# The last step of an inverse transform: one float32 product, or three float32r products of split operands

## The chip, the cores and the metric

The kernel runs on one core of one Trainium2 chip. The core has a matrix engine (TensorE, in the profile PE, with its weight loads shown apart as PEld), a vector engine (DVE), a scalar engine (ACT), GpSimd (POOL) and a sync engine (SP) that here only issues transfers. They run beside each other and wait for each other by semaphores; each works through its own queue in order. The metric is the device time of one execution in microseconds. Before the change it is 2467.11 us, the median of three runs (2465.29 to 2468.96).

## The reference

```python
X = np.fft.rfft(x, axis=1)                 # x: 8 batches x 3008 x 256
Y = X * (filt_r + 1j * filt_i)[None]
y = np.fft.irfft(Y, n=3008, axis=1).astype(np.float32)
t = y.reshape(8 * 3008, 256)
h = t @ w_in                               # 256 x 2048
g = h * (1.0 / (1.0 + np.exp(-1.702 * h)))
out = g @ w_out                            # 2048 x 256
```

A long convolution along the sequence, by a Fourier transform, is followed by a feed-forward block over all 24064 rows.

## The kernel before

The transform of length 3008 = 64 x 47 is done by small matrix products: a step over 64 points, a step over 47 points, the product with the filter, and the two steps back. The 47-point steps read and write the 64-point ones through DRAM, since the data are turned between them. The feed-forward block works on tiles of 512 rows (384 in some tiles that end a batch), six tiles a batch.

The first batch is transformed alone, in float32 (`first_fft`). From then on two things run at once. `mlp(b, t, y, nb)` does the feed-forward block of a tile in 16 steps, one for each 128 of the 2048 hidden channels: six products into a PSUM tile `h` (`first`, line 537), two activations on ACT (`g` and `gh`, lines 541 and 542), a difference on DVE (`gl`, line 543) and six products into two PSUM tiles `o` (`second`, line 551). All of these are float32r products of operands split into a high and a low part, so that each product of two float32 matrices is three float32r products: high by high, low by high, high by low. Beside it a generator `fft(b + 1)` does the transform of the next batch up to the last inverse step, in small pieces handed out between the steps of `mlp`; it is split into high and low parts in the same way, with `mm3` for the three products, and with its steps over 47 points at lines 442 to 445.

The last inverse step, over 64 points, is `signal(b, t, y)`. It makes one tile `y`, already split into high and low, for `mlp`. From the second batch on it loads `br` (128 partitions x 4 x 256) from DRAM (`b_d`, two transfers, one for each half of the partitions). For each half `m` of the 256 columns of `br` it then does four products into one PSUM tile `i1`, one for each of the four pieces of 128 columns, with the table `t2_sb` of 128 x 128 as the moving operand and the piece of `br` as the weights, in float32. In a batch's last tile the fourth product has only 64 rows and 64 columns (line 510). ACT then copies `i1` to the high part of `y` and DVE subtracts to get the low part. In the first batch `br` comes from an on-chip tile `b_t` by four transposes instead of a load.

`signal` yields after each half. The main loop, at the end of the file, advances it after the steps 3 and 9 of the tile before (11 and 13 where that tile ends a batch), and the load goes out with the first half. That order is what the program is written in; a scheduler then orders each engine's queue from it, other than the parts pinned with `keep_in_program_order`, and often moves a half of `signal` as much as two tiles ahead of its use. Tiles in SBUF come from rotating pools: `raw` (six buffers) holds `br` as well as the inputs and intermediate results of `fft`.

Of the kernel before, what the change touches and what calls it, by code (L numbers as in the profile page):

```python
# [9 lines left out]
F32 = mybir.dt.float32  # L10
F32R = mybir.dt.float32r
# [3 lines left out]
ALU = mybir.AluOpType  # L15

B, S, D, DFF = 8, 3008, 256, 2048
N1, N2 = 64, 47
NS = 32
NH = 24  # L20
P = 128
# [129 lines left out]
def tile_kernel(  # L151
# [9 lines left out]
    nc = tc.nc  # L161
    const = ctx.enter_context(tc.tile_pool(name="const", bufs=1))
# [7 lines left out]
    def raw(name):  # L170
        return sb.tile([P, 4, D], F32, tag="raw", name=name, bufs=6)
# [6 lines left out]
    def load_in(dst, src):  # L178

        ins = nc.sync.dma_start(dst, src)  # L180
        if in_order[0]:
            tc.keep_in_program_order(ins)


    tab = const.tile([P, sum(WIDTHS.values())], F32, name="tab")
    t1_sb = const.tile([P, 2, P], F32R, name="t1_sb")
    de_sb = const.tile([Q, 2, 4, Q], F32R, name="de_sb")
    HALF = NFC // 2
    table, at = {}, 0
# [3 lines left out]
    t2_sb, sign = table["t2"], table["sign"]  # L193
# [70 lines left out]
                todo[i - 4].send(to)  # L264
            yield

    b_of, stores, done_w = {}, [], [0]

    zy = []

    def mm3(ps, wh, wl, mh, ml):
        nc.tensor.matmul(ps, wh, mh, start=True, stop=False)  # L272
        nc.tensor.matmul(ps, wh, ml, start=False, stop=False)  # L273
        nc.tensor.matmul(ps, wl, mh, start=False, stop=True)  # L274
# [10 lines left out]
    def split_de():  # L285

        pin = tc.keep_in_program_order
        de_f = table["de"].rearrange("p (m c) -> p m c", m=4)  # L290
        pin(nc.scalar.copy(t1_sb[:, 0], table["t1"]))
        pin(nc.vector.tensor_tensor(t1_sb[:, 1], table["t1"], t1_sb[:, 0].bitcast(F32), ALU.subtract))
        pin(nc.gpsimd.memset(de_sb.bitcast(F32), 0.0))
        for k in range(2):
            h, o = slice(64 * k, 64 * k + 48), slice(64 - 64 * k, 112 - 64 * k)
            pin(nc.scalar.copy(de_sb[h, k, :, h], de_f[h, :, h]))
            pin(nc.vector.tensor_tensor(de_sb[h, k, :, o], de_f[h, :, h], de_sb[h, k, :, h].bitcast(F32), ALU.subtract))
            pin(nc.gpsimd.tensor_copy(de_sb[o, k], de_sb[h, k].bitcast(F32)))
# [190 lines left out]
    def signal(b, t, y):  # L489

        if b:
            br = raw(f"br_{b}_{t}")
            for j in range(2):
                n = NH * j + 4 * t
                load_in(br[64 * j : 64 * j + 64], b_of[b][n : n + 4].rearrange("n k d -> k n d"))
            br = [br[:, :, P * m : P * m + P] for m in range(2)]
        full = 4 if t < 5 else 3
        for m in range(2):
            if b == 0:
                ps = ps_f.tile([P, 4, P], F32, tag="f", name=f"bt_{t}_{m}")  # L500
                for i in range(4):
                    q = 4 * (4 * t + i)
                    nc.tensor.transpose(ps[:, i], b_t[:, m, q : q + 4].rearrange("p c s -> p (c s)"), table["eye"])
                br = {m: sb.tile([P, 4, P], F32, tag="half", name=f"br_{b}_{t}_{m}", bufs=4)}
                (nc.vector.tensor_copy if m else nc.scalar.copy)(br[m], ps)
            ps = ps_f.tile([P, 512], F32, tag="f", name=f"i1_{b}_{t}_{m}")
            for i in range(full):
                nc.tensor.matmul(ps[:, P * i : P * i + P], br[m][:, i], t2_sb, start=True, stop=True)  # L508
            if full == 3:
                nc.tensor.matmul(ps[:, 384:448], br[m][0:64, 3], t2_sb[0:64, 0:64], start=True, stop=True)  # L510
            w = P * full
            to = [(y, 0, w, 0)]
            if full == 3:
                to.append((carry, 0, 64, 384) if b % 2 == 0 else (y, 448, 64, 384))
            for dst, o, w, q in to:
                nc.scalar.copy(dst[:, 0, m, o : o + w], ps[:, q : q + w])
                nc.vector.tensor_tensor(dst[:, 1, m, o : o + w], ps[:, q : q + w], dst[:, 0, m, o : o + w].bitcast(F32), ALU.subtract)
            if full == 3 and b % 2:
                nc.gpsimd.tensor_copy(y[:, :, m, 384:448], carry[:, :, m, :].bitcast(F32))  # L519
            yield  # L520
# [47 lines left out]
    def store():  # L568

        if stores:  # L570
            nc.sync.dma_start(*stores.pop(0))

    def run(gen, n=None):
        while n is None or n > 0:
            if next(gen, run) is run:
                return False
            n = None if n is None else n - 1
        return True


    carry = const.tile([P, 2, 2, 64], F32R, name="carry")
    b_t = const.tile([P, 2, 96, NS], F32, name="b_t")
    ys = {}

    def start(b, t):
        ys[b, t] = sb.tile([P, 2, 2, 512], F32R, tag="y", name=f"y_{b}_{t}")
        return signal(b, t, ys[b, t])
# [7 lines left out]
    for i, (b, t) in enumerate(tiles):  # L595
        if t == 0:

            done, chunk, chunks = 0, 0, 6 * NFC - (18 if b == 0 else 8)
            nxt = fft(b + 1) if b + 1 < B else iter(())
        nb = 4 if t < 5 or b % 2 else 3  # L600
        sig = start(*tiles[i + 1]) if i + 1 < len(tiles) else iter(())
        for fc, _ in enumerate(mlp(b, t, ys.pop((b, t)), nb)):
            if fc == 0:
                store()
            if i == 0:
                run(w_parts, 1)
                if fc == 9:
                    split_de()
                    in_order[0] = False
            if i or fc >= 10:  # L610
                chunk += 1
                while chunk <= chunks and done < STEPS * chunk // chunks:
                    run(nxt, 1)
                    done += 1
            if fc in ((11, 13) if t == 5 else (3, 9)):
                run(sig, 1)
        run(sig)
        if i == 0:
            zy.append(const.tile([P, 4, 2, 2, D], F32R, tag="zy", name="zy"))
            nc.gpsimd.memset(zy[0][32:64].bitcast(F32), 0.0)  # L620
# [29 lines left out]
```

## Time and profile before

| | |
|---|---|
| median of three runs | 2467.11 us |
| profiled execution | 2467.57 us, of which the span from the first to the last instruction is 2465.7 |
| granted clock of TensorE, mean | 0.992 |
| transfers | 246.60 MB, 100 GB/s on average |
| matmuls and weight loads | 11082 each |
| transfers that load `br` | 84, median 4.6 us from issue to landing |

The page gives busy time of each engine, then the chain of work that ended last, then groups of equal instructions. In a row of a group stand the line, the engine, the operation, what it writes and reads, its shape and count; behind the first bar its busy time and the mean length of one; behind the second the idle time of its engine just ahead of it, and who ended most of that idle time. In a row of the timeline stand start and length in microseconds, the engine, the line, the operation and the number of instructions merged into the row. Rows of waits read: who waited for whom, total, times, longest. Rows of windows give a stretch, its length, the busy time of each engine (PE, PEld, DVE, ACT, POOL, with counts), the granted clock, and share and rate of transfers.

### The profile page before, as it was taken

To read this page: it belongs to the slowest core of one execution; us is meant where nothing else is said; L and a number is where in the kernel's file an instruction comes from. 1 tells how busy PE (TensorE), PEld (TensorE's weight loads), DVE (VectorE), ACT (ScalarE), POOL (GpSimd) and SP (SyncE) were. 2 spreads that over 40 slices of the span, in tenths; PEclk is the share of its full clock that TensorE was granted. 3 is DMA by queue.
4 is the path that set the end of the run, shared out by engine and by line. 5 is a ranking of instruction groups with operands and counts; after the bars stand their busy time and mean duration, and the time that the engine had idled before them with its cause. 6 is when DMAs were issued, how large, how long until landed. Compare 5 with 4: busy or idle time off the path is not lost.

```text
span 2465.7 us, 31786 instructions
## 1 busy us (share of the span) xinstructions
PE 2398.9 (97%) x11082; PEld 1986.8 (81%) x11082; DVE 1538.4 (62%) x2167; ACT 1313.0 (53%) x2441; POOL 824.3 (33%) x714
## 2 busy tenths in 40 slices
PE   7789999999999999999999999999999999999999
PEld 6568778877888888988887887988888888898887
DVE  6856884488638883578735786368753788422222
ACT  5555565555555555555554555556555555444443
POOL 4743552355214432344323443234422354000000
PEclk9799999999999999999999999999999999999999
DMA  9335334544345434534344343444335443300000
GB/s 281 95 97 129 92 96 132 132 115 115 91 150 110 100 88 115 142 93 103 96 136 106 93 100 92 137 103 116 88 94 141 100 98 85 70 16 9 18 9 18
DMA packets 140927, 246.60 MB, mean 100 GB/s; under 512 B 15584, under 2 KB 81248, under 8 KB 140768
## 3 DMA queue, kind: packets, MB, share of 16 engines
q1 hardware_dynamic: 62528, 133.72, 19.6%
q10 hardware_dynamic: 53152, 66.80, 10.3%
q0 software_dynamic: 25088, 44.05, 9.2%
q8 instruction: 88, 1.44, 0.2%
q14 instruction: 71, 0.58, 0.1%
HBM read 150.67 MB, written 93.85 MB: 99 GB/s over the span
## 4 chain that ended last, share of the span: by engine, by line
PE 78%; DVE 7%; DMA 5%; issue 2%; ACT 2%; POOL 1%; SPq 1%; ACTq 1%; POOLq 0%; DVEq 0%
PE o L551 35%; PE h L537 35%; PE i L508 3%; DVE gl L543 2%; DMA br<-b_d 2%; PE s L445 2%; PE i L445 2%; DMA x<-in_x_dram 1%; DVE c_buf L396 1%; DMA zy<-a_d 1%; DMA b_d<-b 1%; POOL c_buf L389 1%; PE s L272 1%; PE s L274 1%; PE s L273 1%
## 5 line engine op out<-in xcount | busy, mean ns | idle before, releaser
L537 PE MATMUL h<-y,wi 128*128 128x512 f32 (+1 forms) x4608 | 1172.9, 387 | 2.8 <-ACT gh L542 1.6
L543 DVE TENSOR_TENSOR gl<-g,gh 128x512 fp32r<-128x512 f32 (+1 forms) x768 | 657.2, 858 | 737.7 <-ACT gh L542 653.3
L537 PEld LDWEIGHTS h<-y,wi 128*128 128x128 f32 x4608 | 862.8, 188 | 173.3 <-ACT gh L542 2.5
L541 ACT ACTIVATE g<-h 128x512 f32<-128x512 f32 (+1 forms) x768 | 452.5, 589 | 909.7 <-PE h L537 795.6
L551 PE MATMUL o<-gh,wo 128*128 128x512 f32 (+1 forms) x3072 | 832.5, 390 | 10.9 <-ACT gh L542 9.1
L551 PEld LDWEIGHTS o<-gh,wo 128*128 128x128 f32 x3072 | 571.0, 189 | 130.5 <-ACT gh L542 15.1
L551 PE MATMUL o<-gl,wo 128*128 128x512 f32 (+1 forms) x1536 | 479.9, 388 | 8.9 <-DVE gl L543 8.8
L542 ACT ACTIVATE gh<-h 128x512 fp32r<-128x512 f32 (+1 forms) x768 | 448.5, 585 | 51.4 <-PE o L551 46.5
L460 POOL TENSOR_TENSOR zy<-c_buf,zy 48x512 fp32r<-48x512 f32 x224 | 334.4, 1493 | 96.7 <-DVE zy L459 87.2
L551 PEld LDWEIGHTS o<-gl,wo 128*128 128x128 f32 x1536 | 285.4, 188 | 68.7 <-DVE gl L543 14.6
L389 POOL TENSOR_TENSOR c_buf<-c_buf,u_buf 112x512 f32<-112x512 f32 x128 | 185.2, 1447 | 457.9 <-DVE c_buf L388 456.8
L409 POOL TENSOR_TENSOR xl<-x,xh 128x512 fp32r<-128x512 f32 x84 | 112.3, 1349 | 424.9 <-ACT xh L408 392.9
L428 POOL DMA_DIRECT2D zy<-a_d x224 | 128.3, 575 | 279.6 <-PE s L445 74.9
L396 DVE TENSOR_TENSOR c_buf<-s,c_buf 48x512 f32<-48x512 f32 x224 | 154.1, 688 | 29.4 <-ACT c_buf L395 23.4
L396 DVE TENSOR_TENSOR b<-i,b 48x512 f32<-48x512 f32 x224 | 154.0, 687 | 7.8 <-ACT b L395 1.4
L395 ACT COPY c_buf<-s 48x512 f32<-48x512 f32 x224 | 130.2, 581 | 24.7 <-PE s L445 13.4
L395 ACT COPY b<-i 48x512 f32<-48x512 f32 x224 | 130.1, 581 | 20.8 <-DVE b L396 6.3
L459 DVE CAST zy<-c_buf 48x512 fp32r<-48x512 f32 x224 | 94.2, 421 | 51.9 <-POOL c_buf L389 47.9
L508 PEld LDWEIGHTS i<-tab,br 128*128 128x128 f32 x736 | 101.1, 194 | 26.0 <-issue 8.8
L508 PE MATMUL i<-tab,br 128*128 128x128 f32 x736 | 105.7, 280 | 11.3 <-DMA br<-b_d 7.8
L519 POOL CAST y<-carry 128x128 fp32r<-128x128 f32 x8 | 2.8, 378 | 263.8 <-PE h L537 263.6
L387 DVE TENSOR_TENSOR u_buf<-c_buf,f_buf 48x512 f32<-48x512 f32 x112 | 87.6, 782 | 3.6
(88 smaller groups left out, 1263.4 us busy)
## 6 DMA issues: line engine op xcount, KB each, us to landing
f_buf<-fs SPq DMA_DIRECT2D x224, 192.0 KB, 3.4
zy<-a_d POOLq DMA_DIRECT2D x224, 192.0 KB, 3.6
x<-in_x_dram SPq DMA_DIRECT2D x48, 512.0 KB, 4.8
out_dram<-out SPq DMA_DIRECT2D x44, 512.0 KB, 3.6
a_d<-ah ACTq DMA_DIRECT2D x84, 256.0 KB, 3.5
a_d<-al ACTq DMA_DIRECT2D x84, 256.0 KB, 3.9
b_d<-b ACTq DMA_DIRECT2D x112, 192.0 KB, 2.5
br<-b_d SPq DMA_DIRECT2D x84, 256.0 KB, 4.6
```

The costliest lines, as they stand in the source:

```text
L389: nc.gpsimd.tensor_tensor(u1, u1, u2, ALU.add)
L395: nc.scalar.copy(dst[h], ps[k][o])
L396: nc.vector.tensor_tensor(dst[h], ps[k][h], dst[h], ALU.add)
L409: nc.gpsimd.tensor_tensor(xl, src, xh.bitcast(F32), ALU.subtract)
L428: nc.gpsimd.dma_start(zy[0][64 * k : 64 * k + 48, i % 2].rearrange("p k s d -> p k (s d)"), src.rearrange("n k s d -> n k (s d)"),)
L460: nc.gpsimd.tensor_tensor(y[o, k], u1[h], y[h, k].bitcast(F32), ALU.subtract)
L508: nc.tensor.matmul(ps[:, P * i : P * i + P], br[m][:, i], t2_sb, start=True, stop=True)
L537: nc.tensor.matmul(ps[:, :w], wi_sb[half][:, wk, kc, c], y[:, yk, kc, :w], start=n == 0, stop=n == 5)
L541: nc.scalar.activation(g[:, :w], ps[:, :w], AF.Gelu_apprx_sigmoid)
L542: nc.scalar.activation(gh[:, :w], ps[:, :w], AF.Gelu_apprx_sigmoid)
L543: nc.vector.tensor_tensor(gl[:, :w], g[:, :w], gh[:, :w].bitcast(F32), ALU.subtract)
L551: nc.tensor.matmul(pos[m][:, :w], wo[:, wk, P * m : P * m + P], gp[gk][:, :w], start=fc == 0 and n == 0, stop=fc == NFC - 1 and n == 2,)
```

## The change

From the second batch on, `signal` splits `br` into a high part (a copy to float32r on ACT) and a low part (a subtraction on POOL), for each half of the columns, into `b_hl`, a tile with two places that alternate from tile to tile and that takes the memory of `b_t` once the first batch is done. The table `t2` is split once in the same way (`t2_hl`, in `split_de`). Each of the four products is then `mm3`, three float32r products with 128 columns of the moving operand. In the last tile of a batch the fourth product now uses all 128 rows, and 64 columns, in every batch; in the first batch the products stay float32. `signal` yields once more, behind the load and the split, and the main loop advances it after steps 1, 5 and 9 (9, 12 and 14 where the tile ends a batch).

```diff
+    t2_hl = const.tile([P, 2, P], F32R, name="t2_hl")
...
-        pin(nc.scalar.copy(t1_sb[:, 0], table["t1"]))
-        pin(nc.vector.tensor_tensor(t1_sb[:, 1], table["t1"], t1_sb[:, 0].bitcast(F32), ALU.subtract))
+        for t, name in ((t1_sb, "t1"), (t2_hl, "t2")):
+            pin(nc.scalar.copy(t[:, 0], table[name]))
+            pin(nc.vector.tensor_tensor(t[:, 1], table[name], t[:, 0].bitcast(F32), ALU.subtract))
...
-            br = [br[:, :, P * m : P * m + P] for m in range(2)]
+            if not b_hl:
+                b_hl.append(const.tile([P, 2, 2, 4, D], F32R, tag="b_t", name="b_hl"))
+            hl = b_hl[0][:, t % 2]
+            for m in range(2):
+                ms = slice(P * m, P * m + P)
+                nc.scalar.copy(hl[:, 0, :, ms], br[:, :, ms])
+                nc.gpsimd.tensor_tensor(hl[:, 1, :, ms], br[:, :, ms], hl[:, 0, :, ms].bitcast(F32), ALU.subtract)
+        yield
...
-            for i in range(full):
-                nc.tensor.matmul(ps[:, P * i : P * i + P], br[m][:, i], t2_sb, start=True, stop=True)
-            if full == 3:
-                nc.tensor.matmul(ps[:, 384:448], br[m][0:64, 3], t2_sb[0:64, 0:64], start=True, stop=True)
+            for i in range(4):
+                w = P if i < full else 64
+                if b:
+                    ms = slice(P * m, P * m + P)
+                    mm3(ps[:, P * i : P * i + w], hl[:, 0, i, ms], hl[:, 1, i, ms], t2_hl[:, 0, :w], t2_hl[:, 1, :w])
+                else:
+                    nc.tensor.matmul(ps[:, P * i : P * i + w], br[m][:, i], t2_sb[:, :w], start=True, stop=True)
...
-    b_t = const.tile([P, 2, 96, NS], F32, name="b_t")
+    b_t = const.tile([P, 2, 96, NS], F32, tag="b_t", name="b_t")
...
-            if fc in ((11, 13) if t == 5 else (3, 9)):
+            if fc in ((9, 12, 14) if t == 5 else (1, 5, 9)):
```

Two places show how the instructions stand. The first is PE's queue where the first half of tile (5, 3), that is `i1_5_3_0`, is made, during the feed-forward block of tile (5, 0). Before, with `h` and `o` the two parts of that block and `gh`, `gl` the operands of the second part (batch, tile and step are the first three numbers of a name):

```order
L537 MATMUL h_5_0_15_14357<-y_5_0_13595,wi_1_840 128x512 x6
L551 MATMUL o_5_0_0_13959<-gl_5_0_13_14310,wo_1_841 128x512
L551 MATMUL o_5_0_1_13960<-gl_5_0_13_14310,wo_1_841 128x512
L508 MATMUL i1_5_3_0_14991<-tab_74,br_5_3_14988 128x128 x4
L445 MATMUL i2_6_2_0_15018<-zy_1189,de_sb_76 112x512
```

Now, during the second step of tile (5, 1):

```order
L274 MATMUL i1_5_3_0_15586<-t2_hl_76,b_hl_3367 128x128
L275 MATMUL i1_5_3_0_15586<-t2_hl_76,b_hl_3367 128x128
L273 MATMUL i1_5_3_0_15586<-t2_hl_76,b_hl_3367 128x128
L549 MATMUL h_5_1_2_14955<-y_5_1_14462,wi_0_499 128x512 x6
L274 MATMUL i1_5_3_0_15586<-t2_hl_76,b_hl_3367 128x128
L275 MATMUL i1_5_3_0_15586<-t2_hl_76,b_hl_3367 128x128
L447 MATMUL s2_6_4_0_15620<-zy_1192,de_sb_77 112x512
```

Four float32 products have become twelve float32r products, mostly in one row and here with the six products of a step of `mlp` ahead of the last two; they stand four steps of `mlp` later than before, still well ahead of tile (5, 3).

The second place is where the split of the same `br` stands, in the queues of ACT and POOL. On ACT, where before step 9's activations of tile (5, 0) followed step 8's:

```order
L541 ACTIVATE g_5_0_8_14168<-h_5_0_8_14161 128x512
L542 ACTIVATE gh_5_0_8_14169<-h_5_0_8_14161 128x512
L541 ACTIVATE g_5_0_9_14197<-h_5_0_9_14190 128x512
L542 ACTIVATE gh_5_0_9_14198<-h_5_0_9_14190 128x512
L395 COPY c_buf2_81<-s2_6_2_0_14836 48x512
```

two copies now stand between them:

```order
L554 ACTIVATE gh_5_0_8_14685<-h_5_0_8_14677 128x512
L503 CAST b_hl_3367<-br_5_3_15474 128x4x128 x2
L553 ACTIVATE g_5_0_9_14713<-h_5_0_9_14706 128x512
L554 ACTIVATE gh_5_0_9_14714<-h_5_0_9_14706 128x512
L397 COPY c_buf2_82<-s2_6_2_0_15380 48x512
```

On POOL, two subtractions now stand between the differences of the transform's filter step (`c_buf`, `zy`) and its loads from DRAM:

```order
L391 TENSOR_TENSOR c_buf1_81<-c_buf1_81,u_buf1_84 112x512
L462 TENSOR_TENSOR zy_1192<-c_buf1_81,zy_1192 48x512 x2
L504 TENSOR_TENSOR b_hl_3367<-br_5_3_15474,b_hl_3367 128x4x128 x2
L430 DMA zy_1192<-a_d6_14517 48x2x512 x2
L391 TENSOR_TENSOR c_buf2_82<-c_buf2_82,u_buf0_83 112x512
```

What ACT and POOL do behind these rows now waits for the load of `br`, which before only PE waited for.

More of the change, by code (lines that the diff above doesn't have):

```diff
@@ L265, in weights @@
             yield
-    b_of, stores, done_w = {}, [], [0]
+    b_of, b_hl, stores, done_w = {}, [], [], [0]
     zy = []
```

## The prediction

> **What bounds the kernel now.** I read the page first, from the top: busy time by engine, the chain, the groups.
>
> ```profile
> span 2465.7 us, 31786 instructions
> PE 2398.9 (97%) x11082; PEld 1986.8 (81%) x11082; DVE 1538.4 (62%) x2167; ACT 1313.0 (53%) x2441; POOL 824.3 (33%) x714
> PE 78%; DVE 7%; DMA 5%; issue 2%; ACT 2%; POOL 1%; SPq 1%; ACTq 1%; POOLq 0%; DVEq 0%
> L508 PEld LDWEIGHTS i<-tab,br 128*128 128x128 f32 x736 | 101.1, 194 | 26.0 <-issue 8.8
> L508 PE MATMUL i<-tab,br 128*128 128x128 f32 x736 | 105.7, 280 | 11.3 <-DMA br<-b_d 7.8
> ```
>
> PE is busy 97% of the span and holds 78% of the chain; every other engine has a third of its time or more free. So the question is how many nanoseconds of PE's queue a product takes, and only then who makes PE wait. The waits of PE and of ACT, and the three stages (first transform, body, last batch without transform work), come next.
>
> ```profile
> 0.00:75.00 75.00, 55.78 (x333) 44.27 (x334) 52.04 (x78) 39.69 (x83) 37.81 (x31) 0.91 0.79 239
> 75.00:2115.00 2040.00, 1998.75 (x9146) 1651.05 (x9145) 1388.76 (x1942) 1129.00 (x2086) 785.97 (x682) 0.99 0.43 108
> 2115.00:2465.00 350.00, 344.35 (x1607) 291.44 (x1605) 97.60 (x148) 144.34 (x273) 0.53 (x2) 1.00 0.08 23
> PE o L551 <- ACT gh L542: 9.1, 8, 2.8
> PE i L508 <- DMA br<-b_d: 7.8, 11, 1.5
> ACT g L541 <- PE h L537: 795.6, 595, 5.4
> PE i L445 <- POOL zy L460: 0.8, 1, 0.8
> ```
>
> From 75 us on PE idles 41 us in 2040 and 6 in 350. What is added to PE's queue there is added to the time, nearly one for one. The changed step itself waits for its own load 11 times, 7.8 us in all. ACT, in turn, waits for PE 795.6 us.
>
> **What a product costs on PE.** Mean durations are no use here: records of 280 ns overlap, since eight of them begin within 0.89 us. What counts is the step from one start to the next, read in the timeline (start, length, engine, line, count).
>
> ```profile
> 1119.48 0.97 PEld L508 LDWEIGHTS i<-tab,br 128*128 128x128 f32 x8 [0.72 <-DVE gl L543]
> 1120.37 0.18 PEld L445 LDWEIGHTS s<-zy,de_sb 112*112 112x112 f32 x1
> 1126.93 0.63 PE L445 MATMUL s<-zy,de_sb 112*112 112x512 f32 x2
> 1127.39 1.07 PE L551 MATMUL o<-gh,wo 128*128 128x512 f32 x4
> 1128.31 2.88 PE L537 MATMUL h<-y,wi 128*128 128x512 f32 x12
> 1131.03 0.62 PE L551 MATMUL o<-gl,wo 128*128 128x512 f32 x2
> 1040.20 0.28 PE L442 MATMUL i<-zy,de_sb 112*112 112x256 f32 x1
> 1040.32 0.28 PE L443 MATMUL i<-zy,de_sb 112*112 112x256 f32 x1
> 1040.43 0.28 PE L442 MATMUL i<-zy,de_sb 112*112 112x256 f32 x1
> 1040.55 0.28 PE L443 MATMUL i<-zy,de_sb 112*112 112x256 f32 x1
> 1040.67 1.09 PE L551 MATMUL o<-gh,wo 128*128 128x512 f32 x4
> ```
>
> The four float32 products of one call (four rows of columns) stand in the trace as eight pairs of weight load and matmul: a float32 product is two pairs. Eight loads take 1120.37 - 1119.48 = 0.89 us, 0.111 us a pair, **0.223 us a float32 product**. A float32r product is one pair: with 512 columns (1131.03 - 1128.31)/12 = 0.227 us, with 256 columns (1040.67 - 1040.20)/4 = 0.117 us. No row shows one with 128.
>
> Below, it can't cost less than its columns: 256 more columns cost 0.110 us, so 128 would cost 0.117 - 0.055 = **0.062 us** if columns alone count. Above, I bound it by a whole float32 product of the same shape, 0.223 us. Between these I look for what else paces short matmuls, and find it in the first transform, where float32 pairs have 96 columns only.
>
> ```profile
> 41.18 0.97 PEld L366 LDWEIGHTS i<-tab,c_buf 112*128 112x128 f32 x8
> 42.07 0.28 PEld L359 LDWEIGHTS s<-zs,tab 96*112 96x112 f32 x2
> L537 PEld LDWEIGHTS h<-y,wi 128*128 128x128 f32 x4608 | 862.8, 188 | 173.3 <-ACT gh L542 2.5 <-ACT y L516 1.4 <-POOL wi L239 0.6
> L445 PEld LDWEIGHTS i<-zy,de_sb 112*112 112x112 f32 x210 | 36.7, 175 | 13.7 <-POOL zy L460 3.6 <-issue 1.6
> ```
>
> Those eight pairs take 42.07 - 41.18 = 0.89 us, 0.111 each, exactly what 128 columns take. With a quarter fewer columns they should have taken 0.083. What both have in common is a weight load of 128 columns. So a train of short matmuls goes at the pace of its weight loads, 0.111 us. Is a float32r load quicker? Its record (line 537) is 188 ns long where the float32 one (line 508) is 194, and 16 columns fewer (line 445) save 13 ns, 0.8 ns a column, or 104 ns for 128 columns. Both kinds read four bytes an element and look alike. I take **0.111 us for a float32r product of 128 columns**: half of a float32 product, not a quarter, and there are three of them.
>
> **The change part by part.** One call of the signal step for one half of the columns (84 of them from the second batch on: 7 batches, 6 tiles, 2 halves) goes from 8 pairs to 12.
>
> 70 calls are of full tiles: 12 x 0.1115 - 8 x 0.1115 = 0.446 us more, together **+31.2 us**.
>
> 14 calls are of a batch's last tile, where the fourth product had 64 rows and 64 columns.
>
> ```profile
> 611.18 0.83 PE L508 MATMUL i<-tab,br 128*128 128x128 f32 x6
> 611.94 0.43 PE L510 MATMUL i<-tab,br 64*128 64x64 f32 x2
> 612.30 1.20 PE L551 MATMUL o<-gh,wo 128*128 128x512 f32 x4
> 613.34 0.62 PE L551 MATMUL o<-gl,wo 128*128 128x512 f32 x2
> ```
>
> From 611.18 to 613.34 are 2.16 us; less four steps of 0.227 that leaves 1.25 us, against 0.89 for four whole products: the small one was the dearest. After the change it has all 128 rows, and its three loads are like the others: 12 x 0.1115 = 1.34, so +0.09 x 14 = **+1.3 us**. The first batch gets the full rows too, still in float32: 2 x (0.89 - 1.25) = **-0.7 us**.
>
> The split is new work for ACT and POOL: 84 copies and 84 subtractions of 128x512.
>
> ```profile
> L408 ACT CAST xh<-x 128x512 fp32r<-128x512 f32 x84 | 50.4, 622 | 36.9 <-DMA x<-in_x_dram 27.9 <-issue 8.5 <-PE s L273 0.5
> L409 POOL TENSOR_TENSOR xl<-x,xh 128x512 fp32r<-128x512 f32 x84 | 112.3, 1349 | 424.9 <-ACT xh L408 392.9 <-PE o L551 17.4 <-PE s L274 6.5
> 1039.95 0.60 ACT L541 ACTIVATE g<-h 128x512 f32<-128x512 f32 x1 [1.63 <-PE h L537]
> ```
>
> The same operations exist: 84 x 0.62 = 52 us on ACT and 84 x 1.35 = 113 us on POOL. ACT idles 1.63 us ahead of an activation in a step without copies, so two copies (1.24 us) fit; POOL is at 33%. The program puts the split six steps of the feed-forward loop (some 16 us at 2.72 us a step) ahead of the products. I cost both at nothing; uncovered, the copies would be at most 52 us, and POOL's subtractions hold up the differences behind them in its queue, for which PE waits 0.8 us now, once. The two more operations of the table's split, once, are nothing.
>
> **Waits.** The load is issued earlier, and PE no longer meets it directly: the 7.8 us go. But ACT's copy now waits for the load, and behind it in ACT's queue stand the next two activations, for which PE waits 9.1 us already. The number of loads that come late is the same (11 of 42, 0.71 us each), and ACT's idle time swallows part: between 0 and 7.8 us come back. I take half: **-3.9 us** net. Other steps that the reordering moves are the same instructions, taken at nothing, within a few microseconds.
>
> Sum on the profiled execution (2467.57 us, of which 2465.7 are span; 0.5 above the median of the runs): 2467.6 + 31.2 + 1.3 - 0.7 - 3.9 = 2495.5, so **2496 us**, 1.2% slower.
>
> **The rivals.**
>
> *Short float32r loads are quicker than these rows let me see, and the time ends not slower.* At 0.062 us a pair a full call takes 0.74 where it took 0.89 (-0.148 x 70 = -10.4 us), a last tile's at most 0.74 where it took 1.25 (-0.51 x 14 = -7.1), with -0.7 and -3.9: 2445. It decides at 0.223/3 = 0.074 us a pair. For it: no float32r load stands alone in the trace, all hide behind longer matmuls. Against: the equal lengths of the records.
> The Trainium skill, TensorE: Matmul & The Clock Gate, section on the weight-path perf modes, says that the fast weight load is on for 128 weights where the type is not FP32, and that FP32 gains nothing from it; it doesn't say on which side float32r falls. The 188 against 194 ns speak for FP32's side. The same page, section Back-to-back issue gap, gives about 81 ns a matmul for sustained pairs of load and matmul with 128 columns. By it a call would take 12 x 0.081 = 0.97 us: +5.6 us on the full tiles, -3.9 on the last ones, less 4.6, so an estimate of 2465, no change that can be measured; the float32 pairs here take 0.111.
>
> *A short float32r product costs as much as a float32 one*, my upper bound: 12 x 0.223 = 2.68 us a call, +1.785 x 70 = 125, +1.43 x 14 = 20, less 4.6: 2608. Nothing shows it; the step falls evenly from 512 to 256 columns. But nothing below 256 is shown either.
>
> *The wait moves to ACT and grows.* If all 42 loads come late by the mean of 0.71 us, with the activations behind them, 30 us come back in place of 3.9: 2496 + 3.9 - 7.8 + 30 = 2522. ACT's idle time speaks against it.
>
> **How the numbers follow.** Paced by loads, few waits: 0.60, between 2485 and 2510 (0.108 us a pair gives 3.5 us less, all waits back 4 more, reordering 10 either way). Quick loads: 0.12 (2445 to 2465). As float32: 0.20. Waits on ACT: 0.08, to 2540. The range leaves out only the costly product: 2443 to 2540. Faster by over 0.2% (below 2462; about what a measurement of this kernel can tell from no change) 0.10, most of the quick loads; within 0.2% 0.04; slower 0.86.
>
> **What would show it.** In the profile after: twelve pairs of the signal step from first load to the next line's in 1.34 us (0.74 or 2.68 for the rivals), 1008 pairs in place of 644 and the 28 small ones; their weight loads still near 188 ns; PE's wait for the load gone, ACT's copy waiting for it a few microseconds; POOL some 113 us busier. I am wrong if the twelve take much less or more, or if PE's wait for the activations passes 20 us.

## The result, and the profile after

The changed kernel takes 2524.12 us, the median of four runs (2521.47 to 2528.18), against 2467.47 before in the same set: a ratio of 1.0228, with a 95% interval of 1.0215 to 1.0241. That is 56.7 us more, where the prediction had 28.5 (2496, in a range of 2443 to 2540, slower at 0.86). The sign and the price of the products were right; the loss is twice as large, and lies outside the 2485 to 2510 that the working itself gave.

First the page and the mean clock of the profiled execution after (2522.77 us), and the same three stages as before, with the stage borders where the batches end now.

```profile
span 2521.0 us, 32608 instructions
PE 2444.1 (97%) x11418; PEld 2029.0 (80%) x11418; DVE 1561.3 (62%) x2168; ACT 1353.2 (54%) x2526; POOL 948.5 (38%) x798
core 0: 2521.0 us, clock 0.988
0.00:75.00 75.00, 56.32 (x336) 44.72 (x337) 52.75 (x78) 39.76 (x84) 38.10 (x32) 0.90 0.80 242
75.00:2165.00 2090.00, 2038.42 (x9431) 1687.70 (x9430) 1409.63 (x1943) 1162.92 (x2158) 894.08 (x753) 0.99 0.42 106
2165.00:2521.00 356.00, 349.35 (x1654) 296.58 (x1652) 98.95 (x148) 150.52 (x285) 16.30 (x14) 1.00 0.07 22
```

PE has 336 pairs more (11418 against 11082), which is 1008 less 644 and 28. POOL is 124 us busier, ACT 40, and DVE 23, though DVE was given only one small operation more. The first stage is unchanged. In the body PE now idles 52 us, 10 more than before, and in the last stage 1 more; and the mean clock is 0.988 where it was 0.992: 30 us of full clock lost in place of 20.

The weight loads of one call, in the timeline (start, length, engine, line):

```profile
574.21 0.19 PEld L273 LDWEIGHTS i<-t_hl,b_hl 128*128 128x128 f32 x1
574.45 0.19 PEld L274 LDWEIGHTS i<-t_hl,b_hl 128*128 128x128 f32 x1
574.56 0.19 PEld L275 LDWEIGHTS i<-t_hl,b_hl 128*128 128x128 f32 x1
574.67 0.19 PEld L273 LDWEIGHTS i<-t_hl,b_hl 128*128 128x128 f32 x1
...
575.45 0.19 PEld L274 LDWEIGHTS i<-t_hl,b_hl 128*128 128x128 f32 x1
575.56 0.19 PEld L275 LDWEIGHTS i<-t_hl,b_hl 128*128 128x128 f32 x1
575.67 0.53 PEld L549 LDWEIGHTS h<-y,wi 128*128 128x128 f32 x3
```

From the first load to the next line's are 1.46 us, but the first step, 0.24, still has a matmul of 512 columns beside it. From the second load on are eleven steps in 1.22 us: 0.111 us each. That is the price that the prediction took from the float32 pairs of 96 columns. What was not in it shows in the waits of PE and ACT:

```profile
PE o L563 <- DVE gl L555: 18.3, 16, 3.2
PE o L563 <- ACT gh L554: 11.4, 12, 2.8
PE s L444 <- DMA zy<-a_d: 9.7, 5, 4.3
PE i L273 <- ACT b_hl L503: 5.0, 6, 1.3
ACT b_hl L503 <- DMA br<-b_d: 52.5, 22, 4.1
```

PE's own wait for the load is gone, as forecast. But ACT now waits for it 52.5 us, 2.4 us each time where the prediction took 0.71, and PE waits 18.3 us for the low part `gl`, which DVE makes from what ACT made (8.8 us before). PE's wait for the activation `gh` is 11.4 us (9.1 before).

### The profile page after: what moved, and what is told of

The parts are those of the page before. It is cut to its first block, busy times and chain, and to the rows that moved or that the text cites. A ratio compares the mean times of both kernels' runs of the same rounds, so it can differ in the third digit from the quotient of the medians.

```text
span 2521.0 us, 32608 instructions
## 1 busy us (share of the span) xinstructions
PE 2444.1 (97%) x11418; PEld 2029.0 (80%) x11418; DVE 1561.3 (62%) x2168; ACT 1353.2 (54%) x2526; POOL 948.5 (38%) x798
## 5 line engine op out<-in xcount | busy, mean ns | idle before, releaser
L555 DVE TENSOR_TENSOR gl<-g,gh 128x512 fp32r<-128x512 f32 (+1 forms) x768 | 675.3, 882 | 769.8 <-ACT gh L554 694.2
L563 PE MATMUL o<-gh,wo 128*128 128x512 f32 (+1 forms) x3072 | 833.3, 390 | 11.9 <-ACT gh L554 11.4
L563 PE MATMUL o<-gl,wo 128*128 128x512 f32 (+1 forms) x1536 | 478.7, 388 | 18.3 <-DVE gl L555 18.3
L391 POOL TENSOR_TENSOR c_buf<-c_buf,u_buf 112x512 f32<-112x512 f32 x128 | 193.1, 1509 | 459.0 <-DVE c_buf L390 457.8
L504 POOL TENSOR_TENSOR b_hl<-br,b_hl 128x512 fp32r<-128x512 f32 x84 | 111.7, 1347 | 309.6 <-ACT b_hl L503 303.6
L397 ACT COPY c_buf<-s 48x512 f32<-48x512 f32 x224 | 130.2, 581 | 19.8 <-PE s L445 9.5
L273 PE MATMUL i<-t_hl,b_hl 128*128 128x128 f32 x336 | 88.2, 263 | 5.2 <-ACT b_hl L503 5.0
L275 PE MATMUL i<-t_hl,b_hl 128*128 128x128 f32 x336 | 91.9, 275 | 1.3 <-POOL b_hl L504 1.3
```

The source lines that it names most:

```text
L391: nc.gpsimd.tensor_tensor(u1, u1, u2, ALU.add)
L397: nc.scalar.copy(dst[h], ps[k][o])
L555: nc.vector.tensor_tensor(gl[:, :w], g[:, :w], gh[:, :w].bitcast(F32), ALU.subtract)
L563: nc.tensor.matmul(pos[m][:, :w], wo[:, wk, P * m : P * m + P], gp[gk][:, :w], start=fc == 0 and n == 0, stop=fc == NFC - 1 and n == 2,)
```

## The experiments

All times are medians; ratios are to runs of the kernel before in the same set. The medians of these sets lie between 2467.5 and 2468.9 us, so times of different sets are compared as they are, within a microsecond or so. Two theories for what the pairs leave unexplained: the split's own work and waits, or the new order and the longer trains of products in PE's queue.

**The factors apart.** The float32 products back, no split; the new yields, the earlier load and the full rows stay:

```diff
...
-            for m in range(2):
-                ms = slice(P * m, P * m + P)
-                nc.scalar.copy(hl[:, 0, :, ms], br[:, :, ms])
-                nc.gpsimd.tensor_tensor(hl[:, 1, :, ms], br[:, :, ms], ...)
...
-                    mm3(ps[:, P * i : P * i + w], hl[:, 0, i, ms], hl[:, 1, i, ms], t2_hl[:, 0, :w], t2_hl[:, 1, :w])
+                    nc.tensor.matmul(ps[:, P * i : P * i + w], br[:, i, ms], t2_sb[:, :w], start=True, stop=True)
```

> The changed kernel with its float32 products back and no split; the earlier load, the added yield and the full 128 rows of a last tile's fourth product stay. Theory (a pair of weight load and short matmul takes 0.111 us whatever its type, and the rest of the loss comes from the split's copies and subtractions on ACT and POOL): against the kernel before only gains are left, 16 last-tile calls x 0.36 us = 5.8 us and up to 7.8 us of waits for the load: 2454 to 2463 us. Rival A (the new places of the instructions, not the split, cost the 20 us that the pairs don't explain): about 2480 to 2487.

Measured 2461.42, ratio 0.997 (0.9955 to 0.9985): the new order by itself costs nothing, and rival A falls.

The same with the split kept in the program and its result unused (only the `mm3` line replaced):

> As the run with float32 products and no split, but the split is still done (84 copies on ACT, 84 subtractions on POOL), and its result is not used; the products read the loaded tile in float32. Theory (the split makes the waits): 15 to 25 us above the run without split, 2470 to 2487. Rival B (the waits come of twelve products in a row in PE's queue): the same as without the split, within 4 us.

Measured 2477.02, ratio 1.0034 (1.0022 to 1.0046): 15.6 us for the split alone, at the low end of what was expected.

The three products without the split, from a tile that is set once:

```diff
+                nc.gpsimd.memset(b_hl[0].bitcast(F32), 0.5)
...
-                nc.scalar.copy(hl[:, 0, :, ms], br[:, :, ms])
-                nc.gpsimd.tensor_tensor(hl[:, 1, :, ms], br[:, :, ms], ...)
```

> The changed kernel with the three float32r products, but without the split: the operands are a constant tile that is set once, so the output is not the reference's; the load of the batch's data is still made and nothing reads it. Theory: 84 calls x 4 more pairs x 0.1115 = 37.5 us above the float32 run without split, so 2492 to 2502, and 20 us or more below the changed kernel. Rival B: as the changed kernel, 2515 to 2528.

Measured 2499.2, ratio 1.0123 (1.0107 to 1.0139): 37.8 us above the float32 run, where the working by pairs gives 37.5. (Nothing reads the load here; in the float32 run PE waited 2.0 us for it.)

| | no split | split | difference |
|---|---|---|---|
| float32 products | 2461.4 | 2477.0 | 15.6 |
| three float32r products | 2499.2 | 2524.1 | 24.9 |
| difference | 37.8 | 47.1 | |

Rival B is wrong as it stood: the split costs with short trains too. But it costs 9.3 us more with the long ones. To see where, I sorted PE's time past 80 us of each profiled execution: every step from start to start at its usual size (0.227 us for 512 columns, 0.1735 for 384, 0.118 for 256, 0.1115 for 128 or fewer, and so on), the idle time that some wait ended, half of the time that the clock stood at a half outside these waits (what such a stretch adds), and the rest.

| profiled execution | usual steps | waits | half clock | rest |
|---|---|---|---|---|
| before | 2304.2 | 39.9 | 8.7 | 27.7 |
| float32, no split | 2301.3 | 34.8 | 9.6 | 26.5 |
| float32, split | 2301.3 | 43.2 | 10.9 | 32.3 |
| float32r, no split | 2337.3 | 39.9 | 8.4 | 22.8 |
| changed kernel | 2337.9 | 49.7 | 19.8 | 28.1 |

The products are the first column. The split adds 8 to 10 us of waits with either kind of product, 5 to 6 in the rest, and, with the float32r products only, 11.4 us of half clock.

Each row is one execution, though, and all runs together say less of the half clock. Their mean granted clock is 0.992 without and 0.9905 with the split in float32, and 0.991 and 0.988 with three products: the split loses some 4 us of full clock in the one case and 8 in the other. The profiled executions of the float32 split and of float32r without split had the highest clocks of their runs (0.992; the lowest were 0.989 and 0.990). So the half clock is some 4 of the 9.3 us, not all of them, and the 9.3 is itself uncertain: by the spread of the runs, an estimate, it lies between 3 and 16.

**What paces a short pair.** Second and third products cut to half the columns, with the correction of 64 columns left out:

```diff
+                    nc.tensor.matmul(po, hl[:, 0, i, ms], t2_hl[:, 0, :w], start=True, stop=False)
+                    nc.tensor.matmul(po[:, :w2], hl[:, 0, i, ms], t2_hl[:, 1, :w2], start=False, stop=False)
+                    nc.tensor.matmul(po[:, :w2], hl[:, 1, i, ms], t2_hl[:, 0, :w2], start=False, stop=True)
```

> The changed kernel, with the second and third product of each mm3 of the signal step cut to 64 of the 128 columns (half of the table's correction is left out, so the output is less exact). Paced by weight loads: the same time as the changed kernel within 4 us, and pairs with 64 columns still start 0.111 us apart. Paced by columns (0.43 ns each by the steps at 256 and 512): 644 pairs x 64 columns x 0.43 ns = 18 us less, 2506.

Measured 2526.22, ratio 1.0227 (1.0209 to 1.0244): no gain. Its weight loads in the timeline, where now only every third has 128 columns behind it:

```profile
574.40 0.19 PEld L522 LDWEIGHTS i<-t_hl,b_hl 128*128 128x128 f32 x1
...
575.40 0.19 PEld L522 LDWEIGHTS i<-t_hl,b_hl 128*128 128x128 f32 x1
575.51 0.19 PEld L523 LDWEIGHTS i<-t_hl,b_hl 128*128 128x128 f32 x1
```

Ten steps in 1.11 us again: the columns don't pace the pair. Pairs of 64, 96 and 128 columns all start 0.111 us apart, and what they share is a weight load of 128 columns. That the load paces them, and not another fixed cost of a pair, is the likely reading; no run made the load alone smaller.

**What the split costs by.** In the changed kernel two things stand out. One is a DVE operation beside a subtraction on POOL. First POOL's timeline, then DVE's:

```profile
496.68 2.54 POOL L504 TENSOR_TENSOR b_hl<-br,b_hl 128x512 fp32r<-128x512 f32 x2
500.37 3.12 POOL L462 TENSOR_TENSOR zy<-c_buf,zy 48x512 fp32r<-48x512 f32 x2 [1.14 <-DVE zy L461]
```

```profile
497.15 2.62 DVE L389 TENSOR_TENSOR u_buf<-c_buf,f_buf 48x512 f32<-48x512 f32 x1
500.71 1.66 DVE L388 SCALAR_TENSOR_TENSOR u_buf<-c_buf,f_buf 48x512 f32<-48x512 f32 x1
502.40 1.65 DVE L555 TENSOR_TENSOR gl<-g,gh 128x512 fp32r<-128x512 f32 x1
503.96 0.68 DVE L390 TENSOR_TENSOR c_buf<-c_buf,f_buf 112x512 f32<-112x512 f32 x1
504.57 0.68 DVE L555 TENSOR_TENSOR gl<-g,gh 128x512 fp32r<-128x512 f32 x1
```

An operation of 0.7 us that begins at 497.15 ends at 499.77, 0.55 us behind the end of POOL's two subtractions (499.22). Over the whole trace, the 398 full-size `gl` that overlap no such operation of POOL last 0.69 us in the mean, the 306 that do 1.17. Only 45 of the 306 lie beside a subtraction of the split; the others lie beside POOL's work for the transform. The `gl` at 502.40 is such a one: it overlaps POOL's subtractions for `zy`, which waited for the DVE operations behind the held-up one. Then PE waits:

```profile
499.96 1.52 PE L549 MATMUL h<-y,wi 128*128 128x512 f32 x6
504.10 0.73 PE L563 MATMUL o<-gl,wo 128*128 128x512 f32 x2 [2.61 <-DVE gl L555]
```

The Trainium skill, SBUF — State Buffer, section on the two separate sides, says that DVE and GpSimd share a port pair as a lock, held for a whole instruction, and that a DVE operation with two SBUF inputs needs it. The trace agrees: the operation at 497.15 ends only behind both subtractions. DVE's additions at line 398, which take one of their two inputs from PSUM, are not held up: they last 0.69 us, beside such an operation of POOL (203 of them) or not (245).

The other is ACT's wait for the load, with the activation behind it, at the start of a batch:

```profile
1557.43 0.62 ACT L503 CAST b_hl<-br 128x512 fp32r<-128x512 f32 x1 [4.10 <-DMA br<-b_d]
1557.96 0.59 ACT L553 ACTIVATE g<-h 128x512 f32<-128x512 f32 x1
```

To tell them apart, the low part was moved to DVE (`nc.gpsimd` to `nc.vector` in the subtraction):

> The changed kernel, with the low parts of the split subtracted on DVE in place of POOL (84 x 0.69 us more for DVE, 113 us less for POOL). In the trace of the changed kernel DVE operations that overlap POOL's subtractions last up to 2.6 us where they last 0.7 elsewhere, and the differences gl come late. Theory C (half of the split's cost is DVE held up by POOL's subtractions): 5 to 12 us less than the changed kernel, 2512 to 2519. Theory D (the split costs because ACT's copy waits for the load): the same or slower by DVE's new work, 2522 to 2530.

Measured 2503.27, ratio 1.0143 (1.0127 to 1.0158): 20.9 us less, more than theory C gave, though DVE has 84 operations more. By the same sorting its waits are 37.5 us, 12 less than in the changed kernel, and half clock is 14.7, 5 less. Its waits of ACT and PE, and, in the second fence, those of PE in the run with float32r products and no split:

```profile
ACT b_hl L503 <- DMA br<-b_d: 50.4, 21, 4.2
PE o L563 <- DVE gl L555: 13.2, 17, 3.4
PE o L563 <- ACT gh L554: 11.1, 13, 2.8
```

```profile
PE o L560 <- DVE gl L552: 12.8, 13, 3.9
PE o L560 <- ACT gh L551: 7.4, 7, 2.8
```

ACT waits for the load as long as in the changed kernel, so that wait costs little by itself. PE's wait for `gl` is back where it is without split, from 18.3 us; its wait for `gh`, behind the copies in ACT's queue, stays up. The run also takes the 84 subtractions out of POOL's queue, in which the transform's loads of `zy` stand. PE's wait for these falls from 9.7 to 6.4 us, but it is 9.8 without any split too, so it isn't the split's.

The split one yield behind the load:

```diff
+        yield
+        if b:
             for m in range(2):
                 ms = slice(P * m, P * m + P)
                 nc.scalar.copy(hl[:, 0, :, ms], br[:, :, ms])
...
-            if fc in ((9, 12, 14) if t == 5 else (1, 5, 9)):
+            if fc in ((7, 10, 12, 14) if t == 5 else (1, 4, 7, 10)):
```

> The changed kernel, with one more yield between the load and the split, and the steps 1, 4, 7 and 10 (7, 10, 12 and 14 where a tile ends a batch), so that the load has some three steps of the feed-forward loop (8 us) to land before ACT's copy stands in its queue. Theory D (ACT waits for the load, 22 times and 52 us, with the activations behind it): ACT's wait for the load falls under 10 us, and the time by 10 to 18 us, to 2506 to 2514. Theory C (POOL's subtractions hold up DVE): the time falls by less than 5 us.

Measured 2505.24, ratio 1.015 (1.0134 to 1.0165): 18.9 us less, a little more than theory D gave. But its waits say otherwise:

```profile
ACT b_hl L505 <- DMA br<-b_d: 35.3, 12, 4.1
PE o L565 <- DVE gl L557: 20.7, 21, 3.9
```

ACT still waits 35 us for the load, and PE waits more for `gl` than in the changed kernel. Sorted, its waits are 43.4 us, 6 less, and half clock is 5.0, nearly 15 less. All four runs have a clock of 0.993, where all four of the changed kernel have 0.988, some 12 us. So most of the gain is the clock's, and theory D comes near by luck: the wait that it named went only from 52.5 to 35.3 us.

Then each half of the split by itself. Copies alone (the low part set once):

> The changed kernel without POOL's 84 subtractions: the low part is a constant that is set once, so the output is less exact. What is left of the split is ACT's copies and their wait for the load. The run without any split took 2499, the changed kernel 2524. Theory D (the copies and their wait): 2515 or more. Theory C (POOL's subtractions): 2508 or less. About 2511: both, in halves.

Measured 2504.47, ratio 1.0144 (1.0127 to 1.0161): 5 us above no split. Subtractions alone (the high part set once; contrary to the text, constant and difference still add up to the operand, so the product is formed after all):

> The changed kernel without ACT's 84 copies: the high part is a constant that is set once, and POOL subtracts that constant from the loaded tile, so the output is not the reference's. What is left of the split is POOL's subtractions, and POOL waits for the load. Theory C: 2515 or more. Theory D: 2508 or less.

Measured 2509.5, ratio 1.0166 (1.0151 to 1.0181): 10 us above no split. So 5 and 10 where both make 25: neither theory holds alone, and the halves don't add. Sorted in the same way, the copies alone add no waits to the run without split, and 8 us of half clock (3 by the mean clock of all four runs); the subtractions alone add 6 us of waits and 7 of half clock (6 by all four). Both cures at once:

> Both cures of the split together: low parts on DVE, and the split one yield behind the load. Each alone took about 20 of the split's 25 us away (2503 and 2505, with 2499 for no split at all). If they cure the same loss (few long gaps of PE, each followed by a stretch at half clock): 2496 to 2504, no better than one alone by more than 5 us. If they cured different losses: 2490 or less, below the run without split.

Measured 2503.85, ratio 1.0145 (1.0132 to 1.0158): no better than one. Its waits are 43.8 us and half clock is 6.0. So the two cures took the same loss away, and what is left of the split costs some 5 us.

**The clock behind a gap.** How the clock enters can be seen in the changed kernel. First PE's rows at three waits, then three stretches in each of two places (us from the start, length, busy time of PE, PEld, DVE, ACT and POOL, then the granted clock).

```profile
546.17 0.74 PE L563 MATMUL o<-gl,wo 128*128 128x512 f32 x2 [2.48 <-DVE gl L555]
```

```profile
1558.10 0.33 PE L273 MATMUL i<-t_hl,b_hl 128*128 128x128 f32 x1 [1.33 <-ACT b_hl L503]
...
1559.11 0.33 PE L273 MATMUL i<-t_hl,b_hl 128*128 128x128 f32 x1 [0.57 <-ACT b_hl L503]
```

```profile
540.00:546.00 6.00, 3.70 (x17) 2.73 (x15) 5.88 (x5) 1.09 (x2) 4.34 (x4) 1.00 0.36 37
547.40:550.80 3.40, 3.40 (x9) 2.61 (x9) 2.37 (x3) 0.04 (x1) 2.44 (x2) 0.50 0.45 116
551.00:556.00 5.00, 5.00 (x24) 4.05 (x23) 3.96 (x6) 4.26 (x8) 2.45 (x3) 1.00 0.44 101
```

```profile
1550.00:1557.00 7.00, 6.78 (x30) 5.26 (x29) 1.54 (x3) 2.17 (x4) 0.00 (x0) 1.00 0.54 141
1561.20:1564.50 3.30, 3.30 (x9) 2.58 (x8) 1.73 (x2) 0.23 (x1) 2.86 (x2) 0.50 0.45 126
1565.00:1572.00 7.00, 7.00 (x38) 5.90 (x37) 1.39 (x2) 2.17 (x4) 0.00 (x0) 1.00 0.00 0
```

PE waits 2.5 us for `gl` up to 546.2, and at 547.4 the clock falls to a half for 3.4 us: nine matmuls where 15 would fit. At 1558 it waits 1.3 and 0.6 us for ACT's copies, and the same follows. Behind the gap of 2.6 us at 504.1 nothing follows; not every gap counts. In the run with 64 columns the same two gaps, 2.57 us at 504.1 and 2.48 at 547.8, have it the other way: a stretch follows the first and none the second. Which gap is followed is chance, as far as these traces tell. Of the 19 gaps of over 2.4 us past 200 us in all the profiled executions, 15 have a stretch beginning in them or within 3 us behind them. From 200 us to the last products the kernel before has one such stretch, and the changed kernel six, at 212.9, 547.4, 1352.9, 1561.1, 1656.7 and 1861.5, two of them of 6.8 us. Where one follows, a wait costs 1.7 or 3.4 us beyond its length.

**What is left beats both kernels.** The rows alone, in the kernel before:

```diff
-            for i in range(full):
-                nc.tensor.matmul(ps[:, P * i : P * i + P], br[m][:, i], t2_sb, start=True, stop=True)
-            if full == 3:
-                nc.tensor.matmul(ps[:, 384:448], br[m][0:64, 3], t2_sb[0:64, 0:64], start=True, stop=True)
+            for i in range(4):
+                w = P if i < full else 64
+                nc.tensor.matmul(ps[:, P * i : P * i + w], br[m][:, i], t2_sb[:, :w], start=True, stop=True)
```

> The kernel before, with all 128 rows in the fourth product of a batch's last tile (still 64 columns), and nothing else: the added yield and the new steps are not in it. The working of the prediction: 16 calls x 0.36 us = 5.8 us less, a ratio of 0.9977. If the rows are worth nothing and the run with float32 products and no split gained by its earlier load: 0.9995 to 1.0005.

Measured 2463.4, ratio 0.9983 (0.9975 to 0.9992): 4.8 us.

> The kernel with float32 products, no split, full rows and the earlier load once more, with more rounds, beside the one with the rows alone. Rows and load together: a ratio of 0.996 to 0.998. The load's part is what lies between the two: 0 to 7.8 us.

Measured 2460.61, ratio 0.9971 (0.9959 to 0.9983), 7.6 us below the kernel before. Its waits of PE for the load, and, in the second fence, those of the run with the rows alone:

```profile
PE i L513 <- DMA br<-b_d: 2.1, 3, 1.0
```

```profile
PE i L509 <- DMA br<-b_d: 8.5, 10, 1.6
```

6.4 us of waits gone gave 2.8 us by the medians, and the two intervals overlap: the load's gain is likely, not certain. This version, the change without its split and its products, is the fastest of all that ran.

## Why the prediction came out as it did

**Right: the price of a pair.** 0.111 us was taken from float32 pairs of 96 columns and from load records of equal length; the trace after shows 0.111, the run with 64 columns shows that the columns of such short pairs don't matter, and the factors give 37.8 us for the products where the working gives 84 x 4 x 0.1115 = 37.5. The rival with quick loads (0.062) and the one as dear as float32 (0.223) are both out. So is, for these pairs, the figure of about 81 ns in the Trainium skill, TensorE: Matmul & The Clock Gate, section Back-to-back issue gap; they take 111. That the load sets this pace was argued from what short pairs have in common, and is still argued.

**Right: the rows.** 16 x 0.36 = 5.8 us foreseen, 4.8 measured, with 2.0 to 6.2 by the interval.

**Wrong: "I cost both at nothing"**, said of the split's work on ACT and POOL. It costs 24.9 us (2524.1 against 2499.2), which is the gap between 2496 and the measured time but for some 3 us. Those are no more than the runs' own spread, or the term "-3.9 us net" for the waits: PE's own wait for the load did go, but with it went no more than 2.8 us by the medians of the runs with and without the earlier load, and in the changed kernel the other waits grow by more. Three things were missing in that step.

- The copies' cover was judged by ACT's idle time between activations. But ACT runs its queue in order, and the program puts the copy right behind the load: it stood still 2.4 us a time, not 0.71. The six steps of cover that the prediction names are the mean of four and eight (three and five where a tile ends a batch), and they lie between the split and the products; between the load and the copy there are none. The rival "the wait moves to ACT and grows" had this mechanism, at 2522 and a chance of 0.08. That it comes within 2 us of the measurement is luck: the copies with their wait cost 5 us alone, and ACT's wait of 50 us stayed in the run that is 20.9 us faster.
- POOL's subtractions were taken to hold up only POOL's queue. They also hold up DVE, and DVE makes `gl`, for which PE waits (18.3 us, 12.8 without split). This could have been read before: there too, a `gl` beside such an operation of POOL lasts 1.18 us (268 of them), and 0.69 otherwise (436). The subtractions alone cost 10 us.
- A gap of PE was priced at its length. In the changed kernel 11 us more than before are half clock behind such gaps, as much as the waits themselves grew (9.8); the clocks of all runs, 0.988 against 0.992 in the mean, say the same.

**Half luck: the range.** 2524 lies in 2443 to 2540 only because the range took in the rival of waits on ACT, up to 2540, at 0.08; the range's own main part, 2485 to 2510 at 0.60, missed it. Neither of the two named signs of being wrong showed: the twelve pairs start 0.111 us apart as foreseen, and PE waits 11.4 us for the activations, under 20. The wait that grew most was the one for `gl`, which no sign watched, and ACT's wait for the load was to be "a few microseconds".

What stays open is why the same split costs 9 us more with the float32r products, if it does by that much. Two of the six stretches of half clock follow PE's wait for the copies, which the float32 products, reading the loaded tile itself, don't have; one follows `gl`, three the transform's own loads, and no run tells whether the longer trains of short pairs bring these on or the places where the gaps happen to fall.

## What to carry to other kernels

Compare products by pairs of weight load and matmul: with 128 columns or fewer and 128 columns of weights a pair of four-byte operands costs 0.111 us here, so three float32r pairs can't beat the two pairs of one float32 product. With 512 columns it is the other way: a float32 product of 512 columns in the first transform of the kernel before (line 359, 112 columns of weights) takes 0.87 us, from 42.16 to the next line's start at 43.03, and three float32r pairs take 3 x 0.227 = 0.68.

A copy that waits for a transfer belongs behind the transfer by its landing time in the queue of an engine that others wait for; one yield between them gave 18.9 us here, most of it by the clock. Price a new gap of TensorE with the half clock that may follow it, and work for POOL with the DVE operations that it holds up; moving the subtractions to DVE itself gave 20.9 us.

## What was not expected of the hardware

The clock falls to a half behind gaps of PE as short as 2.5 us (at 546.2), or 2.0 (up to 212.6, where a stretch begins at 212.9), and behind 1.3 and 0.6 us close to each other (at 1558), for 3.4 us or twice that. The Trainium skill, TensorE: Matmul & The Clock Gate, section on why this matters for your kernels, warns of gaps above some 3 us; here shorter ones did it.

A float32 product of 64 rows and 64 columns behind others of 128 rows costs 0.36 us more than a whole one of 128 x 128, by the timeline of the kernel before that the prediction shows; using all 128 rows gave 4.8 us over 16 of them.
